# Sixty-four-row products among products of four column chunks, and GELU turned by transposes

## The chip, the cores and the metric

The kernel runs on one core of a Trainium2 chip. The metric is the device time of one execution in microseconds (us); lower is better. The engines of a core run side by side: TensorE (PE in the profile, its weight loads are PEld), VectorE (DVE), ScalarE (ACT), GpSimd (POOL) and SyncE (SP), which here issues all transfers.

## The reference, cut to what matters

One decode step for four tokens of width 448: an attention block over a cached window, then an MLP. All numbers are float32.

```python
x = A_x                                              # (4, 1, 448)
h = x + attention(layernorm(x), k_cache, v_cache, wq, wo)   # last 1024 of 4096 keys, 16 heads, 8 kv heads
y = layernorm(layernorm(h))
u = gelu(y @ w1 + b1)                                # (4, 1792), tanh form
out = h + u @ w2 + b2                                # (4, 448)
```

## The kernel before, in words

The host packs all weights and caches so that SP can fetch them in the order of their use as a few large transfers (`LOADS`, then `v7`, `wo67`, `w1`, `w2`, `w2_low`), into a ring of three buffers. The order of TensorE's instructions is that of the program text; the other engines' queues follow the program's order too, with semaphores between engines set by the tile framework.

For each of the eight key-value heads the kernel projects the queries (`project_q`), forms scores (`scores`), turns the exponentials (`transpose_p`), multiplies with the values (`values`) and adds the head's output to the output projection (`project_o`). After the last head only four rows of 448 numbers are left, and the MLP works on them in a layout of its own: a matrix with four rows is cut into four chunks of columns, chunk j stands on partitions 32 j to 32 j + 31, and of each such 32 partitions every eighth (GAP) carries a token. A product for chunk j thus writes 32 partitions of PSUM only and uses 32 columns of TensorE's array; products for four chunks can be under way at one time. Each float32 product appears in the trace as two passes (a transpose as one), so counts of matmuls there are twice those in the program.

The MLP's steps, with their lines:

- L452 to L457: `pu`, the product of the normalized tokens with w1, four row blocks (a = 0 to 3) times four chunks (j). The block a = 3 has only 64 rows.
- L468, L469: scale and bias on DVE and GELU on ACT, in two parts of the columns (256 and 192), result in `u` (128 x 448).
- L471: five matmuls on zeros (`keep_warm`), which only keep TensorE busy.
- L472 to L476: `put`, five products of column blocks of `u` with `rows_of`, which picks from the identity the 16 partitions that carry tokens. This turns GELU's result from rows into columns. The last 64 columns go to both halves of the partitions.
- L477 to L480: four DVE copies bring `put` into `gT`, where every eighth column of a block of 32 carries a token and the rest stay zero. `gT[:, c]` is the stationary operand for chunk c of w2's rows.
- L481 to L496: `py`, the product with w2. Chunks c = 0 to 10 with four column chunks j each (L486); then four products of 64 rows (L489), whose weights came by `w2_low` and all of which write column chunk j = 3 (`py[3 * Q :, 0, :]`); then chunks c = 11 to 13 (L493), of which c = 12 and 13 have three column chunks only.
- L498, L499: `res`, the sum with the residual on DVE, and the transfer of the result.

w2 comes in five pieces (L374 to L380): chunks 0 to 7 (1792 KB), chunks 8 to 10 (672 KB), the two `w2_low` halves, chunks 11 and 12 (416 KB), chunk 13 (192 KB).

Of the kernel before, what the change touches and what calls it, by code (L numbers as in the profile page):

```python
# [8 lines left out]
F32 = mybir.dt.float32  # L9
# [6 lines left out]
B, D = 4, 448  # L16
# [4 lines left out]
P = 128  # L21
H = P // 2
ND = 4
NKC = W // P
NFC = F // P
FQ = F // 4
Q = 32
# [37 lines left out]
W2L = NFC * D - 2 * (D - DW)  # L65
# [4 lines left out]
def block_kernel(ctx: ExitStack, tc, first, streams, v7, wo67, w1, w2, w2_low, out):  # L70
    nc = tc.nc
# [3 lines left out]
    once = ctx.enter_context(tc.tile_pool(name="once", bufs=1))  # L75
# [3 lines left out]
    ps_m = ctx.enter_context(tc.tile_pool(name="ps_m", bufs=2, space=PSUM))  # L79
# [51 lines left out]
    ident = const.tile([P, P], F32, name="ident")  # L131
# [27 lines left out]
    rows_of = ident.rearrange("p (j b e) -> p j b e", j=4, b=B)[:, :, :, 0]  # L159
# [3 lines left out]
    gT = const.tile([P, NFC + 2, Q], F32, name="gT")  # L163
# [7 lines left out]
    def spread(t):  # L171
        return t[..., ::GAP]
# [43 lines left out]
    def scores(g):  # L216
        s = [ps_s.tile([P, 512], F32, tag="s", name=f"s{g}_{h}") for h in range(2)]
        mx = work.tile([P, 2], F32, tag="mx", name=f"mx{g}")
        for h in range(2):
            for c in range(2):  # L220
                for b in range(B):
                    nc.tensor.matmul(  # L222
                        s[h][b * Q : (b + 1) * Q, :], qT[g % 2][:, c, b, :], load_k(g, h, c)[:, b, :],
                        start=(c == 0), stop=(c == 1),
                    )
            nc.vector.reduce_max(mx[:, h : h + 1], s[h], axis=AX.X)  # L226
        nm = work.tile([P, 1], F32, tag="nm", name=f"nm{g}")
        nc.vector.tensor_max(nm, mx[:, 0:1], mx[:, 1:2])
        nc.vector.tensor_scalar_mul(nm, nm, -SCALE)  # L229
        p = work.tile([P, 2 * 512], F32, tag="p", name=f"p{g}")  # L230
        sums = work.tile([P, 2], F32, tag="sums", name=f"sums{g}")
        for h in range(2):
            nc.scalar.activation(  # L233
                p[:, h * 512 : (h + 1) * 512], s[h], AF.Exp, bias=nm, scale=SCALE,
                accum_out=sums[:, h : h + 1],
            )
        rec = work.tile([P, 1], F32, tag="rec", name=f"rec{g}")
        nc.vector.tensor_add(rec, sums[:, 0:1], sums[:, 1:2])
        nc.vector.reciprocal(rec, rec)
        return p, rec  # L240
# [30 lines left out]
    def columns(t, j):  # L271
        if j < 3:
            return t[:, j * P : (j + 1) * P].rearrange("p (i c) -> p i c", i=2)
        return t[:, None, 3 * P :].to_broadcast([t.shape[0], 2, H])

    def heads(g, po, rec):
        o = work.tile([P, 2, DH], F32, tag="o", name=f"o{g}")
        nc.vector.tensor_scalar_mul(o[:, :, :P], po[:, :, :P], rec)  # L278
        nc.scalar.mul(o[:, :, P:], po[:, :, P:], rec)  # L279
        pt = ps_m.tile([P, 512], F32, tag="m", name=f"pot{g}")  # L280
        if g in (HKV - 3, HKV - 1):
            keep_warm(3 if g == HKV - 1 else 5, pt)
        for c in range(2):
            for i in range(2):
                at = (2 * i + c) * P - i * REP
                nc.tensor.transpose(pt[:, at : at + P], o[:, i, c * P : (c + 1) * P], ident)  # L286
        if g >= HKV - 2:
            keep_warm(1)
        dst = oT[g % 2].rearrange("p (r c) (b e) -> p r (c b) e", r=REP, b=B)[..., 0]
        src = pt.rearrange("p (i k q) -> p q k i", i=2, q=Q)[:, :REP]  # L290
        nc.vector.tensor_reduce(dst, src, axis=AX.X, op=ALU.add)
# [57 lines left out]
    p, rec = scores(0)  # L349
    project_q(1, wq_parts(part("q", 1)))  # L350
    transpose_p(0, p)
    for g in range(HKV):
        if g + 1 < HKV:
            p, rec_next = scores(g + 1)
            if g == HKV - 2:
                heads(g - 1, *late)
            if g + 2 < HKV:
                project_q(g + 2, wq_parts(part("q", g + 2)))
            transpose_p(g + 1, p)
            if g + 1 == HKV - 1:  # L360
                keep_warm(2, ps_m.tile([P, 512], F32, tag="m", name="wait"))
                tail.append(ps_t.tile([P, 2, 512], F32, tag="t", name="tail"))
                keep_warm(5)
        else:
            v7t = load_v7()
            tw = slot("w1")
            wo_last = [wo_rows(tw[:, i * WC : (i + 1) * WC]) for i in range(2)]
            nc.sync.dma_start(tw[:, : 2 * WC], wo67)
            tw1 = tw[:, 2 * WC : 2 * WC + W1C]
            for a, n in ((0, 2 * F), (2 * F, W1C - 2 * F)):  # L370
                nc.sync.dma_start(tw1[:, a : a + n], w1[:, a : a + n])
            tw2 = slot("w2")
            at = 0
            for n in (8 * D, 3 * D, 0, D + DW, DW):  # L374
                if n:
                    nc.sync.dma_start(tw2[:, at : at + n], w2[:, at : at + n])
                else:
                    for h in range(2):
                        nc.sync.dma_start(tw2[h * Q : (h + 1) * Q, W2L : W2L + 4 * H], w2_low[h, :, : Q // 8, :])
                at += n  # L380
        if g == HKV - 1:
            keep_warm(5)
        po = values(g, v7t if g == HKV - 1 else None)
        if g == HKV - 2:
            project_o(g - 1, wo_rows(part("o", g - 1)))
        if g == HKV - 3:
            late = po, rec
        else:
            heads(g, po, rec)
        if g < HKV - 3:  # L390
            project_o(g, wo_rows(part("o", g)))
        if g == HKV - 2:
            accs = once.tile([P, D], F32, tag="u", name="accs")
            nc.scalar.copy(accs, acc)
            hsum = ps_s.tile([P, 512], F32, tag="s", name="hsum")[:, :P]
            ph = hsum.rearrange("p (i c) -> p i c", i=2)
            pu = ps_s.tile([P, 512], F32, tag="s", name="pu")[:, :FQ]
            for j in range(4):
                nc.tensor.matmul(ph[j * Q : (j + 1) * Q], sel, columns(accs, j), start=True, stop=False)
        if g == HKV - 1:  # L400
            keep_warm(5)
            for i in range(2):
                project_o(HKV - 2 + i, wo_last[i])
        if g + 1 < HKV:
            rec = rec_next

    w1t = [tw1[:, a * F : (a + 1) * F] for a in range(3)] + [tw1[:, 3 * F :]]
    w2t = [tw2[:, c * D - max(c - 12, 0) * (D - DW) :][:, : D if c < 12 else DW] for c in range(NFC)]
# [21 lines left out]
    m = row_mean(hs, pm[:, 0:1], "m")  # L430
# [8 lines left out]
    m = row_mean(ds, pm2[:, 0:1], "m2")  # L439
# [8 lines left out]

    r1 = stat("r1")
    s = stat("r2")  # L450
    u = once.tile([P, FQ], F32, tag="u", name="u")
    for a in range(ND):  # L452
        for j in range(4):
            rows, w = w1_part(a, j)
# [14 lines left out]
        nc.scalar.activation(u[:, cols], u[:, cols], AF.Gelu_apprx_tanh)  # L469

    keep_warm(5)  # L471
    put = ps_m.tile([P, 4, 4, B], F32, tag="m", name="put")  # L472
    for c in range(3):
        nc.tensor.matmul(put[:, c], u[:, c * P : (c + 1) * P], rows_of, start=True, stop=True)
    for rows in (slice(0, H), slice(H, P)):
        nc.tensor.matmul(put[rows, 3], u[:, 3 * P :], rows_of, start=True, stop=True)  # L476
    dst = gT[:, :12, :].rearrange("p (c j) q -> p c j q", c=3)  # L477
    nc.vector.tensor_copy(spread(dst), put[:, :3])
    for i, rows, at in ((0, slice(0, H), 12), (1, slice(H, P), 12), (1, slice(0, H), NFC)):
        nc.vector.tensor_copy(spread(gT[rows, at : at + 2, :]), put[rows, 3].rearrange("p (j i) q -> p j i q", i=2)[:, :, i, :])  # L480
    py = ps_o.tile([P, 2, H], F32, tag="o", name="py")  # L481
    for c in range(11):
        for j in range(4):
            n = 2 if c == 0 or j < 3 else 1
            w = columns(w2t[c], j) if n == 2 else w2t[c][:, None, 3 * P :]
            nc.tensor.matmul(py[j * Q : (j + 1) * Q, :n, :], gT[:, c, :], w, start=(c == 0), stop=False)  # L486
    for i, c in enumerate((12, NFC, 13, NFC + 1)):
        w = tw2[:H, W2L + i * H : W2L + (i + 1) * H]
        nc.tensor.matmul(py[3 * Q :, 0, :], gT[:H, c, :], w, start=False, stop=False)  # L489
    for c in range(11, NFC):  # L490
        for j in range(4 if c == 11 else 3):
            w = columns(w2t[c], j) if j < 3 else w2t[c][:, None, 3 * P :]
            nc.tensor.matmul(  # L493
                py[j * Q : (j + 1) * Q, : 2 if j < 3 else 1, :], gT[:, c, :], w,
                start=False, stop=(c == NFC - 1 or j == 3),
            )  # L496
    res = once.tile([P, P], F32, tag="res", name="res")
    nc.vector.tensor_add(res, py.rearrange("p i c -> p (i c)"), hb)  # L498
    nc.sync.dma_start(out, res)  # L499
# [70 lines left out]
```

## Time and profile before

| | |
|---|---|
| median of 3 runs | 214.32 us (214.21 to 214.32) |
| the profiled execution | 214.25 us |
| its span in the profile | 212.5 us |
| TensorE busy (matmuls) | 143.2 us, 67% of the span |
| DVE, ACT, POOL busy | 36.8, 24.5, 5.0 us |
| share of the span on the chain that ended last | DMA 73%, PE 23%, DVE 1%, ACT 1% |
| moved from memory | 88.23 MB, 416 GB/s over the span |

The span reaches from the first to the last instruction of the profiled execution. Engines overlap, so their busy times don't add up to the span; the chain that ended last is followed back from the last instruction to what released it, step by step, and its shares do add up. The busy time of a matmul in the profile is from its start to the modelled end of its result, so matmuls in a stream overlap each other, and what one costs in a stream is the step from one start to the next.

### The profile page before, as it was taken

The page shows a single profiled execution, that of the slowest core. Times are in us where ns is not written, and L with a number is a line of the kernel's source. Part 1 is how long each engine was busy: PE and PEld are TensorE (multiplying, and loading weights), DVE is VectorE, ACT ScalarE, POOL GpSimd, SP SyncE. Part 2 cuts the span into 40 slices and gives each one's busy share as a digit, 9 for nine tenths or more (in the row PEclk, how much of TensorE's full clock was granted, in tenths as well). Part 3 has the DMA queues.
Part 4 walks back from the last instruction along what each step waited for, and adds up shares of the span by engine and source line. Part 5 has one row for each costly group of instructions (what it writes and reads, how often), then busy time and mean ns, then how long its engine had stood idle before and what let it go on. Part 6 is the DMA issues. An engine that isn't in the chain of part 4 may idle for free.

```text
span 212.5 us, 2534 instructions
## 1 busy us (share of the span) xinstructions
PE 143.2 (67%) x1095; PEld 56.4 (27%) x1095; DVE 36.8 (17%) x152; ACT 24.5 (12%) x58; POOL 5.0 (2%) x16
## 2 busy tenths in 40 slices
PE   0468805862861884870793780685599998999994
PEld 0332301220110521320122220141134433325453
DVE  1521400320130100310122011031032041101220
ACT  2011300210011100200003000030012002100310
POOL 5100000000000000000000000000000000000100
PEclk9999975896797579996589698599589999999999
DMA  7999899999989999899999989899999999999991
GB/s 297 436 406 509 361 489 435 406 445 397 489 375 474 445 395 462 375 503 410 424 456 403 467 382 478 364 479 450 421 435 421 423 414 412 410 432 424 421 383 43
DMA packets 3259, 88.44 MB, mean 416 GB/s; under 512 B 369, under 2 KB 689, under 8 KB 1073
## 3 DMA queue, kind: packets, MB, share of 16 engines
q1 hardware_dynamic: 3248, 88.30, 96.8%
q8 instruction: 8, 0.13, 0.2%
q14 instruction: 3, 0.02, 0.0%
HBM read 88.23 MB, written 0.07 MB: 416 GB/s over the span
## 4 chain that ended last, share of the span: by engine, by line
DMA 73%; PE 23%; SPq 1%; DVE 1%; issue 1%; ACT 1%; ACTq 0%
DMA stream<-stream 60%; DMA w<-w 12%; PE s L222 7%; PE po L261 4%; PE wait L346 3%; PE acc L296 2%; PE py L486 1%; PE pu L455 1%; PE pq L199 1%; PE pot L286 1%; PE ppt L247 1%; PE tail L346 1%; DVE o L278 0%; SPq L98 0%; PE py L493 0%
## 5 line engine op out<-in xcount | busy, mean ns | idle before, releaser
L222 PE MATMUL s<-stream,qT 128*32 128x512 f32 x256 | 37.5, 730 | 17.4 <-DMA stream<-stream 16.8
L261 PE MATMUL po<-stream,pT 128*32 128x512 f32 x224 | 31.7, 703 | 17.3 <-DMA stream<-stream 17.3
L222 PEld LDWEIGHTS s<-stream,qT 128*32 128x32 f32 x256 | 9.9, 132 | 42.6 <-issue 30.4
L226 DVE TENSOR_REDUCE mx<-s 128x1 f32<-128x512 f32 x16 | 11.1, 692 | 57.5 <-PE s L222 57.5
L199 PE MATMUL pq<-stream,yT 128*32 128x512 f32 (+1 forms) x80 | 10.2, 604 | 9.5 <-DMA stream<-stream 6.6
L261 PEld LDWEIGHTS po<-stream,pT 128*32 128x32 f32 x224 | 7.0, 124 | 35.1 <-DMA stream<-stream 20.2
L201 ACT COPY qs<-pq 128x512 f32<-128x512 f32 x8 | 4.7, 586 | 83.1 <-PE pq L199 83.1
L278 DVE TENSOR_SCALAR o<-po,rec 128x256 f32<-128x256 f32 x8 | 3.9, 484 | 59.9 <-PE po L261 59.9
L279 ACT ACTIVATE o<-po,rec 128x256 f32<-128x256 f32 x8 | 3.8, 474 | 74.2 <-DVE o L278 74.2
L233 ACT ACTIVATE p<-s,nm 128x512 f32<-128x512 f32 x16 | 10.9, 690 | 10.0 <-DVE nm L229 10.0
L247 PE MATMUL ppt<-ident,p 128*128 128x128 f32 x64 | 11.1, 303 | 0.4
L296 PE MATMUL acc<-stream,oT 128*32 128x448 f32 x48 | 7.3, 683 | 5.1 <-DMA stream<-stream 3.9
L207 PE MATMUL pqt<-ident,qs 128*128 128x128 f32 x32 | 6.1, 323 | 5.5 <-ACT qs L201 5.5
L286 PE MATMUL pot<-ident,o 128*128 128x128 f32 x32 | 7.2, 317 | 3.6 <-DVE o L278 3.1
L346 PEld LDWEIGHTS <-idle 128*32 128x32 bf16 x71 | 6.4, 96 | 9.4 <-issue 3.6
L199 PEld LDWEIGHTS pq<-stream,yT 128*32 128x32 f32 x80 | 4.2, 125 | 16.9 <-issue 15.7
L247 PEld LDWEIGHTS ppt<-ident,p 128*128 128x128 f32 x64 | 7.6, 152 | 3.7 <-ACT p L233 3.7
L346 PE MATMUL tail<-idle 128*32 128x512 bf16 x29 | 7.6, 381 | 0.0
L286 PEld LDWEIGHTS pot<-ident,o 128*128 128x128 f32 x32 | 3.4, 149 | 13.2 <-DVE o L278 10.5
L346 PE MATMUL wait<-idle 128*32 128x512 bf16 x30 | 6.8, 379 | 0.0
L207 PEld LDWEIGHTS pqt<-ident,qs 128*128 128x128 f32 x32 | 3.9, 160 | 10.2 <-ACT qs L201 8.5
L193 POOL TENSOR_TENSOR r<-ve_r,mhalf 128x1 f32<-128x1 f32 x2 | 1.1, 545 | 191.0 <-DVE ve_r L192 191.0
(118 smaller groups left out, 75.3 us busy)
## 6 DMA issues: line engine op xcount, KB each, us to landing
stream<-stream SPq DMA_DIRECT2D x5, 7040.0 KB, 37.2
stream<-stream SPq DMA_DIRECT2D x3, 6912.0 KB, 39.3
stream<-stream SPq DMA_DIRECT2D x2, 4992.0 KB, 16.0
stream<-stream SPq DMA_DIRECT2D x1, 7168.0 KB, 40.1
w<-w SPq DMA_DIRECT2D x2, 1792.0 KB, 22.4
v<-v SPq DMA_DIRECT2D x1, 3072.0 KB
w<-wo SPq DMA_DIRECT2D x1, 1792.0 KB, 19.5
w<-w SPq DMA_DIRECT2D x1, 1344.0 KB, 26.2
```

Source lines behind the costliest of these rows:

```text
L199: nc.tensor.matmul(pq[j * Q : (j + 1) * Q, cols], yT[:, a, :], w, start=True, stop=True)
L201: nc.scalar.copy(qs, pq)
L207: nc.tensor.transpose(pt[:, i * P : (i + 1) * P], qs[:, i * P : (i + 1) * P], ident)
L222: nc.tensor.matmul(s[h][b * Q : (b + 1) * Q, :], qT[g % 2][:, c, b, :], load_k(g, h, c)[:, b, :], start=(c == 0), stop=(c == 1),)
L226: nc.vector.reduce_max(mx[:, h : h + 1], s[h], axis=AX.X)
L233: nc.scalar.activation(p[:, h * 512 : (h + 1) * 512], s[h], AF.Exp, bias=nm, scale=SCALE, accum_out=sums[:, h : h + 1],)
L247: nc.tensor.transpose(pt[:, c, :], p[:, c * P : (c + 1) * P], ident)
L261: nc.tensor.matmul(po[b * Q : (b + 1) * Q], pT[g % 2][:, c, b, :], vt[:, :, b, :], start=(c == 0), stop=(c == NKC // 2 - 1),)
L278: nc.vector.tensor_scalar_mul(o[:, :, :P], po[:, :, :P], rec)
L286: nc.tensor.transpose(pt[:, at : at + P], o[:, i, c * P : (c + 1) * P], ident)
L296: nc.tensor.matmul(acc[i * Q : (i + 1) * Q, :], oT[g % 2][:, i, :], wt[:, i, :], start=(g == 0), stop=(g == HKV - 3),)
L346: nc.tensor.matmul(to[:Q, :512], idle[:, :Q], idle, start=True, stop=True)
```

## The change: what it does

Two edits in the MLP's second half, and a buffer made to fit.

First, `u` becomes 128 x 512, its last 64 columns set to zero by POOL (the earlier tile `accs`, which shares its buffer, grows with it). The five products with `rows_of` become five transposes against the identity: three into `put`, and two of 128 columns each into a second tile `put2`, the second of them 64 columns further left, so that the last 64 columns of `u` come out on either half of the partitions. The four copies to `gT` now pick every eighth column of the transposes, and the first of them reads `put` alone.

Second, the four 64-row products no longer stand in one block between chunks 10 and 11. One of them follows the product for j = 1 in each of the chunks c = 8, 9, 10 and 11, ahead of those for j = 2 and 3. The products for the chunks themselves are the same.

```diff
--- before.py
+++ after.py
@@ -390,7 +390,7 @@
         if g < HKV - 3:
             project_o(g, wo_rows(part("o", g)))
         if g == HKV - 2:
-            accs = once.tile([P, D], F32, tag="u", name="accs")
+            accs = once.tile([P, 4 * P], F32, tag="u", name="accs")[:, :D]
             nc.scalar.copy(accs, acc)
             hsum = ps_s.tile([P, 512], F32, tag="s", name="hsum")[:, :P]
             ph = hsum.rearrange("p (i c) -> p i c", i=2)
@@ -448,7 +448,8 @@
 
     r1 = stat("r1")
     s = stat("r2")
-    u = once.tile([P, FQ], F32, tag="u", name="u")
+    u = once.tile([P, 4 * P], F32, tag="u", name="u")
+    nc.gpsimd.memset(u[:, FQ:], 0.0)
     for a in range(ND):
         for j in range(4):
             rows, w = w1_part(a, j)
@@ -469,31 +470,31 @@
         nc.scalar.activation(u[:, cols], u[:, cols], AF.Gelu_apprx_tanh)
 
     keep_warm(5)
-    put = ps_m.tile([P, 4, 4, B], F32, tag="m", name="put")
+    put = ps_m.tile([P, 3 * P], F32, tag="m", name="put")
     for c in range(3):
-        nc.tensor.matmul(put[:, c], u[:, c * P : (c + 1) * P], rows_of, start=True, stop=True)
-    for rows in (slice(0, H), slice(H, P)):
-        nc.tensor.matmul(put[rows, 3], u[:, 3 * P :], rows_of, start=True, stop=True)
+        nc.tensor.transpose(put[:, c * P : (c + 1) * P], u[:, c * P : (c + 1) * P], ident)
+    put2 = ps_m.tile([P, 2 * P], F32, tag="m", name="put2")
+    for i in range(2):
+        nc.tensor.transpose(put2[:, i * P : (i + 1) * P], u[:, 3 * P - i * H : 4 * P - i * H], ident)
     dst = gT[:, :12, :].rearrange("p (c j) q -> p c j q", c=3)
-    nc.vector.tensor_copy(spread(dst), put[:, :3])
-    for i, rows, at in ((0, slice(0, H), 12), (1, slice(H, P), 12), (1, slice(0, H), NFC)):
-        nc.vector.tensor_copy(spread(gT[rows, at : at + 2, :]), put[rows, 3].rearrange("p (j i) q -> p j i q", i=2)[:, :, i, :])
+    nc.vector.tensor_copy(spread(dst), put.rearrange("p (c j b e) -> p c j b e", c=3, j=4, b=B)[..., 0])
+    halves = put2.rearrange("p (s j i b e) -> p s i j b e", s=2, j=2, i=2, b=B)[..., 0]
+    for side, i, rows, at in ((0, 0, slice(0, H), 12), (1, 1, slice(H, P), 12), (0, 1, slice(0, H), NFC)):
+        nc.vector.tensor_copy(spread(gT[rows, at : at + 2, :]), halves[rows, side, i])
     py = ps_o.tile([P, 2, H], F32, tag="o", name="py")
-    for c in range(11):
-        for j in range(4):
+    low = list(enumerate((12, NFC, 13, NFC + 1)))
+    for c in range(NFC):
+        for j in range(4 if c < 12 else 3):
             n = 2 if c == 0 or j < 3 else 1
             w = columns(w2t[c], j) if n == 2 else w2t[c][:, None, 3 * P :]
-            nc.tensor.matmul(py[j * Q : (j + 1) * Q, :n, :], gT[:, c, :], w, start=(c == 0), stop=False)
-    for i, c in enumerate((12, NFC, 13, NFC + 1)):
-        w = tw2[:H, W2L + i * H : W2L + (i + 1) * H]
-        nc.tensor.matmul(py[3 * Q :, 0, :], gT[:H, c, :], w, start=False, stop=False)
-    for c in range(11, NFC):
-        for j in range(4 if c == 11 else 3):
-            w = columns(w2t[c], j) if j < 3 else w2t[c][:, None, 3 * P :]
             nc.tensor.matmul(
-                py[j * Q : (j + 1) * Q, : 2 if j < 3 else 1, :], gT[:, c, :], w,
-                start=False, stop=(c == NFC - 1 or j == 3),
+                py[j * Q : (j + 1) * Q, :n, :], gT[:, c, :], w,
+                start=(c == 0), stop=(c == NFC - 1 or (c == 11 and j == 3)),
             )
+            if j == 1 and 8 <= c < 12:
+                i, at = low.pop(0)
+                w = tw2[:H, W2L + i * H : W2L + (i + 1) * H]
+                nc.tensor.matmul(py[3 * Q :, 0, :], gT[:H, at, :], w, start=False, stop=False)
     res = once.tile([P, P], F32, tag="res", name="res")
     nc.vector.tensor_add(res, py.rearrange("p i c -> p (i c)"), hb)
     nc.sync.dma_start(out, res)
```

## Rows read from the trace of the kernel before

**Rows 1.** Busy time of each engine, granted clock and DMA, by stretch of the end.
```profile
core 0: us, PE busy (x) PEld busy (x) DVE busy (x) ACT busy (x) POOL busy (x), PEclk, DMA share, GB/s
...
205.70:208.29 2.59, 2.53 (x88) 2.36 (x89) 0.34 (x2) 0.00 (x0) 0.00 (x0) 1.00 0.65 248
208.29:208.85 0.56, 0.56 (x11) 0.47 (x8) 0.00 (x0) 0.00 (x0) 0.00 (x0) 1.00 0.00 0
```
**Rows 2.** From the end of the chain that ended last: start, duration, step.
```profile
175.10 26.18 DMA w<-w
...
201.33 1.84 PE pu L455 x16
```
**Rows 3.** Timeline from GELU to the first product with w2.
```profile
203.83 0.69 ACT L469 ACTIVATE u<-u 128x256 f32<-128x256 f32 x2 [3.69 <-DVE u L468]
204.30 0.84 PE L474 MATMUL put<-ident,u 128*128 128x16 f32 x6
...
205.41 0.24 DVE L478 COPY gT<-put 128x48 f32<-128x48 f32 x1 [1.29 <-PE put L476]
205.54 0.54 DVE L480 COPY gT<-put 64x8 f32<-64x8 f32 x3
...
205.76 2.60 PE L486 MATMUL py<-w,gT 128*32 128x128 f32 x88 [0.39 <-DVE gT L480]
```
**Rows 4.** SP's issues of three pieces of w2, in narrow windows.
```profile
184.19 0.81 SPq L376 DMA_DIRECT2D w<-w  x2
...
189.50 0.33 SPq L376 DMA_DIRECT2D w<-w  x1
...
193.79 0.33 SPq L376 DMA_DIRECT2D w<-w  x1
```
**Rows 5.** The same three issues by size, with us from issue to landing.
```profile
w<-w SPq DMA_DIRECT2D x1, 1792.0 KB, 21.4
...
w<-w SPq DMA_DIRECT2D x1, 416.0 KB, 18.8
...
w<-w SPq DMA_DIRECT2D x1, 192.0 KB, 15.0
```
**Rows 6.** POOL's memset of gT, and the readers of accs: duration min/median/max ns, start.
```profile
L167 POOL MEMSET gT<- x1: 526/526/526, 2.9 to 2.9; 128x512 f32 x1
...
L399 PE MATMUL hsum<-accs,sel x8: 272/273/297, 185.0 to 185.3; 128*32 128x128 f32 x8
```
**Rows 7.** Timeline of four transposes of an earlier stage and their reader.
```profile
159.14 0.66 PE L207 MATMUL pqt<-ident,qs 128*128 128x128 f32 x4 [0.15 <-ACT qs L201]
...
159.83 0.23 DVE L210 TENSOR_REDUCE q<-pqt 128x16 f32<-128x64 f32 x1 [1.19 <-PE pqt L207]
```
**Rows 8.** Timeline around the 64-row block, in narrow windows.
```profile
208.09 0.27 PE L486 MATMUL py<-w,gT 128*32 128x128 f32 x1
...
208.29 0.30 PE L489 MATMUL py<-w,gT 64*32 64x64 f32 x2
...
208.71 0.22 PE L489 MATMUL py<-w,gT 64*32 64x64 f32 x1
208.85 0.31 PE L493 MATMUL py<-w,gT 128*32 128x128 f32 x4
...
209.76 0.29 DVE L498 TENSOR_TENSOR res<-py,hb 128x128 f32<-128x128 f32 x1 [3.69 <-PE py L493]
```
**Rows 9.** The last products by tile: duration min/median/max in ns, start.
```profile
L493 PE MATMUL py<-w,gT x20: 219/273/297, 208.9 to 209.4; 128*32 128x128 f32 x18, 128*32 128x64 f32 x2
```
**Rows 10.** Timeline of w1's last products, in narrow windows.
```profile
201.33 0.58 PE L455 MATMUL pu<-w,zT 128*32 128x448 f32 x4 [0.52 <-DMA w<-w]
...
201.73 0.56 PE L455 MATMUL pu<-w,zT 128*32 128x448 f32 x4
...
202.22 0.13 PEld L455 LDWEIGHTS pu<-w,zT 64*32 64x32 f32 x5 [0.73 <-issue]
```
**Rows 11.** The block's wait instruction in TensorE's queue: duration ns, start us.
```profile
L489 PEldq EVENT_SEMAPHORE  x1: 51/51/51, 207.5 to 207.5; - x1
```

## The prediction, on record before the result

> **What bounds the kernel now.** I read the chain that ended last first, then its end on the timeline, then the transfers that reach into that end, and at last single instructions in narrow windows. The chain's shares (DMA 73%, PE 23%) say that most of the span is transfers, but the change touches only the last 6 us. There the table by stretch [rows 1] should be read for two things: the granted clock is 1.00 (the 2.4 GHz level) throughout, and the transfers are still at 0.65 of the engines while w2's products run, and at 0.00 afterwards. So TensorE sets the end, but it starts into data that is only just arriving. On the chain [rows 2] w1's last piece lands at 175.10 + 26.18 = 201.28 and its product starts 0.05 later. Then follow GELU, the turn into columns, the copies, and the products with w2 from 205.76 [rows 3]. The profile puts that last start down to the DVE copy, done at 205.41 + 0.24 = 205.65. But w2's first piece was issued at 184.19 and took 21.4 us, so it landed at 205.59 [rows 4, 5]. Two waits end within 0.06 us of each other; removing one leaves the other.
>
> **The edit to GELU's turn.** It replaces five products (ten passes, 204.30 to the copy at 205.41) by five transposes. Four transposes of this shape took 0.66 us to the last result and their reader started 0.69 after the first [rows 7]; three can't take longer. The third needs GELU's second part, done at 203.83 + 0.69 = 204.52, hence ready for TensorE at about 204.57, when two of the transposes are through anyway. The first copy could then start by 204.30 + 0.69 = 204.99, take 0.24 (48 elements per partition, as now), and let TensorE go 0.11 after its end (205.65 to 205.76 now): 205.34, 0.42 us earlier than now. The copy now reads one element in eight; even at twice its price the start would be 205.58. Both lie ahead of w2's first piece at 205.59. So the products start 0.05 after the landing, at 205.64, at the earliest, and not later than now; I take 205.69, a little after the earliest since the queue handles several waits in turn. **Gain: 0.07 us, bounds 0 and 0.12**, of an apparent 0.4. The last three copies (0.54 together) end before 206.2 and serve products after 207.7: hidden. The memset on POOL waits for the readers of accs, which start by 185.3; 512 columns took 0.53 us there, 64 can't take more, and `u` isn't written before w1's products end, after 201.33 [rows 2, 6]. It costs nothing; if it ran late, POOL's power for the norm would queue behind it, by at most 0.53. No transfer is moved.
>
> **The edit to the 64-row products.** First the steps of a stream. From the first product at 205.76 to the start of the last 128-row pass at 208.09 lie 21 steps of a pass of four chunks (11 chunks, two passes each); the first pass after a restart takes 297 ns where the others take 273 [rows 9], so that one step is 0.024 longer: (2.33 - 0.024) / 21 = 0.11 us a step, 0.22 a chunk [rows 3, 8].
>
> Now the block [rows 8]. The last 128-row pass starts at 208.09, the first 64-row pass at 208.29: 0.20, which is 0.09 more than a step. The first two 64-row passes end at 208.29 + 0.30 = 208.59, a pass lasts 0.22, so the second starts at 208.37: 0.08. The other six steps run to 208.71: 0.057 each. Then the next 128-row pass starts at 208.85: 0.14, again 0.09 more than a step, and its own first step is 0.024 longer. Each change between 128 and 64 rows thus costs about 0.09 of standing and 0.024 of restart. No wait explains it: the wait for the two `w_low` pieces was passed at 207.5 [rows 11]. The same shows where no semaphore stands at all, in w1's product: the second 128-row pass follows the first by 0.40 (201.33 to 201.73, with a restart in it), the first 64-row pass follows after 0.49 [rows 10], 0.09 more than even a restarted step and 0.11 more than a plain one.
>
> The block as it is costs 208.85 - 208.09 = 0.76, less the 0.11 step that would stand there anyway, plus 0.024: **0.67 us** for one pair of changes and eight passes. Strewn, each of the four products brings its own pair: 0.20 + 0.08 + 0.14 + 0.024 - 0.11 = 0.334; four cost **1.34**. Net **+0.67**.
>
> Second, the order. The strewn product stands after j = 1, so the chunks' passes are cut into groups: {8: j0 j1}, then {8: j2 j3, 9: j0 j1}, {9, 10}, {10, 11}, and what is left of 11 with 12 and 13. Four products on four different column chunks start within 0.02 us of each other after a restart (four are under way in the row at 208.85), so I take it that those of two neighbouring chunks pair up likewise. Ahead of the last strewn product then stand eight full groups, one half and three mixed: twelve of 0.22 where eleven stand now, **+0.22**. Behind it the longest line is j = 2 of chunks 11, 12, 13, three products, as now (208.85 to 209.76 for DVE's sum).
>
> As a clock: first product 205.69; second pass of {8: j0 j1} at 205.69 + 0.024 + 17 x 0.11 = 207.58; each strewn product moves on by 0.20 + 0.08 + 0.14 to the next group's first pass, and that group's second pass comes 0.134 later, so the groups start at 208.00, 208.55, 209.11 and 209.66; 0.91 later DVE sums at 210.57, against 209.76. Chunk 11, needed at 209.11, has landed at 189.50 + 18.8 = 208.30, chunk 13 at 193.79 + 15.0 = 208.79 [rows 4, 5]: neither is waited for.
>
> **Sum:** -0.07 + 0.67 + 0.22 = +0.82 us. The profiled execution took 214.25 us, 1.75 of it outside its span: 215.07. Its time is 0.07 below the median shown, so I predict **215.1 us**.
>
> The Trainium skill, in TensorEngine Tiling, section Key Properties, says that changing the tiling mode, not just the tile, drains TensorE; the trace agrees, with 0.09 at each change [rows 8, 10]. TensorE: Matmul & The Clock Gate, section Single matmul latency, has a drain at about 175 ns; as an estimate from that page, six more changes at 0.175 would make 1.05, and the sum +1.20, 215.45 us. I keep the price of the rows.
>
> **The rivals.**
> *The strewn products run beside the others* (the other side). The column chunk j = 3 has half as many columns as the others, so it has about 0.11 us to spare in each chunk's 0.22, and a 64-row product needs 0.11. If a change of rows let the other column chunks run on and cost nothing itself, the products would vanish into that gap. Chunk 11 would be reached at 205.69 + 0.024 + 22 x 0.11 = 208.13, before its landing at 208.30; from 208.35 two chunks lead to 208.79, where chunk 13 has just landed; its first pass at 208.84 leaves 0.45 to DVE's sum, as now (0.91 less two chunks): 209.29, 0.47 earlier, **213.8 us**. w2's arrival, not TensorE, then sets the gain. For it: four chunks do run side by side. Against: both places where the row count changes stand still for 0.09, and it decides at that price being zero; at about 0.13 us in all per strewn product it breaks even. Chance 0.10. TensorE: Matmul & The Clock Gate, Part 3: Packing small matmuls, has tiles of the array run at the same time and weight loads pulled ahead where row groups don't conflict, which would favour this rival; at 208.29 the trace shows the contrary [rows 8].
>
> *Only column chunk 3 stands.* The strewn products cost 0.334 each there, the other chunks run on: chunk 3 ends its stream at 205.69 + 0.024 + 8 x 0.22 + 4 x (0.11 + 0.334) = 209.25, its last pass starts 0.06 before. Now the last pass starts at 208.85 + 0.024 + 5 x 0.11 = 209.42, 0.34 ahead of DVE's sum; so the sum comes at 209.53, 0.23 earlier, **214.0 us**. Against it speaks that the block's exit stops the passes of all four. Chance 0.06.
>
> *The halves don't pair up.* If j2 j3 of one chunk and j0 j1 of the next run one after the other, each of four groups takes one to two more steps: 0.44 to 0.88 more, 215.5 to 216.0, **215.7 us**. For it: the four now starting together belong to one chunk; against: the streams of the column chunks drift apart freely. Chance 0.14.
>
> **How the numbers follow.** The forecast has 0.70; its own range is 214.8 to 215.4 (start bounds, roundings of 0.01 in some twenty steps, 0.1 between executions). A measurement of this kernel can tell about 0.2%, 0.43 us, from no change: 213.89 to 214.75. Slower: 0.70 + 0.14 = 0.84. Rival one lies at the edge, half of it counts as faster (0.05), half as same; rival two is same with a little faster: same 0.10, faster 0.06. Range 214.5 to 215.8: it holds the forecast and most of the 0.14, and leaves out both rivals below and the end of the third.
>
> **What would show it.** Right: the first product with w2 at about 205.7, put down to w2's transfer or close behind its landing, with TensorE idle for 0.3 us or more before it; four 64-row products each with 0.20 before and 0.14 behind; DVE's sum near 210.6. Wrong: 64-row passes that overlap those of other chunks in time with no gap before them; a first start well before 205.6, which would mean that w2 landed earlier than its row says; or a granted clock below 1.00 in the last 5 us, where it has been 1.00 so far.

## The result, and the profile after

The changed kernel takes 215.18 us (median of 6, 215.14 to 215.33) against 214.32 us (median of 6, 214.21 to 214.5): 1.0039 times as long, 95% interval 1.0029 to 1.005. That is slower by 0.86 us, where 0.8 was forecast. Its profiled execution took 215.22 us with a span of 213.4.

The end of its timeline (start, duration, engine, line, operation, count, idle time before and what ended it) answers to [rows 3, 8]; lines from L452 on have moved by one or more.

```profile
204.37 0.60 PE L475 MATMUL put<-ident,u 128*128 128x128 f32 x3
...
205.00 0.24 DVE L480 COPY gT<-put 128x48 f32<-128x48 f32 x1 [0.81 <-PE put L475]
205.22 0.55 DVE L483 COPY gT<-put 64x8 f32<-64x8 f32 x3
...
205.80 2.16 PE L490 MATMUL py<-w,gT 128*32 128x128 f32 x68 [0.62 <-DVE gT L483]
207.89 0.13 PEld L497 LDWEIGHTS py<-w,gT 64*32 64x32 f32 x2 [0.20 <-issue]
207.89 0.30 PE L497 MATMUL py<-w,gT 64*32 64x64 f32 x2
208.12 0.16 PEld L490 LDWEIGHTS py<-w,gT 128*32 128x32 f32 x8
208.12 0.43 PE L490 MATMUL py<-w,gT 128*32 128x128 f32 x8
208.47 0.14 PEld L497 LDWEIGHTS py<-w,gT 64*32 64x32 f32 x2 [0.20 <-issue]
...
209.06 0.14 PEld L497 LDWEIGHTS py<-w,gT 64*32 64x32 f32 x2 [0.20 <-issue]
...
209.64 0.13 PEld L497 LDWEIGHTS py<-w,gT 64*32 64x32 f32 x2 [0.20 <-issue]
...
209.86 0.84 PE L490 MATMUL py<-w,gT 128*32 128x128 f32 x16
210.74 0.29 DVE L499 TENSOR_TENSOR res<-py,hb 128x128 f32<-128x128 f32 x1 [4.97 <-PE py L490]
```

Two things are to be seen. The transposes are through early: the first copy starts 0.63 after the first transpose (205.00 - 204.37), where the products took 1.11 [rows 3], but the first product with w2 comes at 205.80, no earlier than before. And the weight loads of the four 64-row products each stand 0.20 us with no wait behind it ("issue"), where one load did before, that of the block:

```profile
208.29 0.19 PEld L489 LDWEIGHTS py<-w,gT 64*32 64x32 f32 x3 [0.20 <-issue]
```

The period from one strewn product to the next is 0.58. From the first product to DVE's sum it is now 210.74 - 205.80 = 4.94 us, where it was 209.76 - 205.76 = 4.00.

By stretch, granted clock and transfers (columns as in [rows 1]):

```profile
205.80:207.89 2.09, 2.09 (x68) 1.89 (x68) 0.00 (x0) 0.00 (x0) 0.00 (x0) 1.00 0.73 277
207.89:209.86 1.97, 1.97 (x34) 1.01 (x32) 0.00 (x0) 0.00 (x0) 0.00 (x0) 1.00 0.07 26
```

The clock stays at 1.00. In the stretch of the strewn products TensorE's matmuls look fully busy (1.97 of 1.97), although seven of the eight changes between 128 and 64 rows, each with its gap, lie in it: their modelled ends overlap the gaps. The weight loads show it: 1.01 of 1.97, where they were 1.89 of 2.09.

### The profile page after: what moved, and what is told of

Its sections match the earlier page's. It is cut to its first block, busy times and chain, and to the rows that moved or that the text cites. A ratio compares the mean times of both kernels' runs of the same rounds, so it can differ in the third digit from the quotient of the medians.

```text
span 213.4 us, 2526 instructions
## 1 busy us (share of the span) xinstructions
PE 143.6 (67%) x1090; PEld 55.7 (26%) x1090; DVE 36.9 (17%) x152; ACT 24.5 (11%) x58; POOL 5.2 (2%) x17
## 4 chain that ended last, share of the span: by engine, by line
DMA 72%; PE 22%; DVE 3%; ACT 1%; issue 1%; SPq 0%; ACTq 0%
DMA stream<-stream 57%; DMA w<-w 12%; PE s L222 5%; PE po L261 5%; PE pq L199 2%; DMA stream<-first 2%; PE py L490 2%; PE pqt L207 1%; PE acc L296 1%; PE pu L456 1%; PE ppt L247 1%; ACT qs L201 1%; PE tail L346 1%; DVE o L278 0%; ACT o L279 0%
## 5 line engine op out<-in xcount | busy, mean ns | idle before, releaser
L222 PE MATMUL s<-stream,qT 128*32 128x512 f32 x256 | 38.1, 741 | 20.4 <-DMA stream<-stream 19.8
L261 PE MATMUL po<-stream,pT 128*32 128x512 f32 x224 | 29.5, 663 | 15.4 <-DMA stream<-stream 15.4
L199 PE MATMUL pq<-stream,yT 128*32 128x512 f32 (+1 forms) x80 | 11.2, 657 | 9.6 <-DMA stream<-stream 6.7
L210 DVE TENSOR_REDUCE q<-pqt 128x16 f32<-128x64 f32 x8 | 1.8, 225 | 19.2 <-PE pqt L207 19.2
```

Source lines behind the costliest of these rows:

```text
L199: nc.tensor.matmul(pq[j * Q : (j + 1) * Q, cols], yT[:, a, :], w, start=True, stop=True)
L222: nc.tensor.matmul(s[h][b * Q : (b + 1) * Q, :], qT[g % 2][:, c, b, :], load_k(g, h, c)[:, b, :], start=(c == 0), stop=(c == 1),)
L261: nc.tensor.matmul(po[b * Q : (b + 1) * Q], pT[g % 2][:, c, b, :], vt[:, :, b, :], start=(c == 0), stop=(c == NKC // 2 - 1),)
```

## The experiments

All ran beside the kernel before on the same chip; the medians given for it are of the same session. A ratio is the time over that of the kernel before, with its 95% interval. The edits are shown shortened, with "..." where code is left out.

**The strewn products alone.** The kernel before with only the second edit.

```diff
-    for c in range(11): ...; the block of four; for c in range(11, NFC): ...
+    for c in range(NFC): ...
+            if j == 1 and 8 <= c < 12:   # one 64-row product
```

> The strewn products alone, GELU turned by products with selectors as before. My theory: the whole loss is here, +0.9 us against the kernel before (0.67 for three more pairs of changes between 128 and 64 rows, 0.22 for the chunk cut in halves): 215.2 us. Rival: the transposes or their strided copies bear part of the loss: well below 215.2, towards 214.3 us if they bear all of it.

Measured: 215.32 us against 214.33, ratio 1.0046 (1.0034 to 1.0059). From the first product to DVE's sum 4.94 us, as in the changed kernel (its lines L487 and L496):

```profile
205.87 2.16 PE L487 MATMUL py<-w,gT 128*32 128x128 f32 x68 [0.39 <-DVE gT L480]
...
210.81 0.29 DVE L496 TENSOR_TENSOR res<-py,hb 128x128 f32<-128x128 f32 x1 [4.62 <-PE py L487]
```

The whole loss is in this edit.

**The transposes alone.** The changed kernel with the block of the kernel before.

```diff
-            if j == 1 and 8 <= c < 12: ...
+    for i, c in enumerate((12, NFC, 13, NFC + 1)):   # the block, between chunks 10 and 11
```

> The transposes alone, the 64-row products in one block as before. My theory: the first product with w2 waits for w2's first piece, so the earlier copies buy next to nothing: first product 0.10 to 0.15 us behind the landing, time 214.25 to 214.32 us. Rival: the turn was the bound, and the products start 0.4 us earlier: 213.9 us.

Measured: 214.36 us against 214.33, ratio 0.9999 (0.999 to 1.0008): no difference that can be told. On its timeline the first copy ends at 205.10 + 0.24 = 205.34 and the first product, which reads it, starts at 205.88, 0.54 later:

```profile
205.10 0.24 DVE L480 COPY gT<-put 128x48 f32<-128x48 f32 x1 [0.82 <-PE put L475]
205.32 0.55 DVE L483 COPY gT<-put 64x8 f32<-64x8 f32 x3
...
205.88 2.60 PE L489 MATMUL py<-w,gT 128*32 128x128 f32 x88 [0.60 <-DVE gT L483]
```

Something other than that copy holds it.

**The last three copies on ACT.** The profile names the last DVE copy (L483) as what the first product waited for, and it does end 0.01 to 0.03 us ahead of it, although chunk 0 doesn't read it.

```diff
-        nc.vector.tensor_copy(spread(gT[rows, at : at + 2, :]), halves[rows, side, i])
+        nc.scalar.copy(spread(gT[rows, at : at + 2, :]), halves[rows, side, i])
```

> The changed kernel with the last three copies to gT on ACT instead of DVE, so that DVE is done 0.5 us earlier. My theory: the first product with w2 stays 0.13 us behind the landing of w2's first piece, time 215.2 us. Rival: the profile is right to name the last DVE copy as what it waits for, and the first product comes up to 0.1 us earlier against the landing.

One execution: 215.34 us. With these three copies gone from DVE the chain of this kernel runs through w2's transfer:

```profile
184.37 21.41 DMA w<-w
205.79 0.14 issue
205.92 2.16 PE py L490 x47
```

The first product stands 0.13 us behind the landing. In the changed kernel it is the same: issued at 184.27, 21.4 under way, 205.67; first product at 205.80.

```profile
184.27 0.33 SPq L376 DMA_DIRECT2D w<-w  x1
...
w<-w SPq DMA_DIRECT2D x1, 1792.0 KB, 21.4
```

So it is w2's first piece that holds the start, and the name in the wait was a coincidence of 0.03 us.

**The strewn products at the ends of chunks.**

```diff
-            if j == 1 and 8 <= c < 12:
+            if j == 3 and 7 <= c < 11:
```

> The changed kernel with each 64-row product behind the last product of a chunk (7, 8, 9, 10) instead of in the middle of one. My theory: the four pairs of changes stay, the cut group goes, so the products from first to DVE's sum take 0.22 us less than in the changed kernel: 214.95 us. Rival: the column chunks drift across the cut at no cost, the whole loss is in the changes: as the changed kernel, 215.2 us.

Measured: 214.94 us, ratio 1.0031 (1.002 to 1.0043). Its TensorE timeline, with DVE's sum:

```profile
207.52 0.30 PE L497 MATMUL py<-w,gT 64*32 64x64 f32 x2
207.74 0.42 PE L490 MATMUL py<-w,gT 128*32 128x128 f32 x8
208.09 0.30 PE L497 MATMUL py<-w,gT 64*32 64x64 f32 x2
...
210.38 0.29 DVE L499 TENSOR_TENSOR res<-py,hb 128x128 f32<-128x128 f32 x1 [4.75 <-PE py L490]
```

The first product is at 205.64, so first product to sum is 4.74 us: 0.20 less than in the changed kernel, 0.74 more than in the kernel before. The cut chunk cost 0.20, three more pairs of changes 0.74. The medians differ by 0.24, in the same direction; the intervals of the two ratios overlap, so it is the profile, one execution of each, that tells them apart.

**The same places, without a change of rows.** The weights' other 64 rows are set to zero, so each product reads 128 rows and adds nothing more.

```diff
+            nc.gpsimd.memset(tw2[H:, W2L : W2L + 4 * H], 0.0)
...
-                w = tw2[:H, W2L + i * H : W2L + (i + 1) * H]
-                nc.tensor.matmul(py[3 * Q :, 0, :], gT[:H, at, :], w, start=False, stop=False)
+                w = tw2[:, W2L + i * H : W2L + (i + 1) * H]
+                nc.tensor.matmul(py[3 * Q :, 0, :], gT[:, at, :], w, start=False, stop=False)
```

> The changed kernel, strewn in the same places, but each of the four products reads 128 rows: the lower 64 rows of its weights are zeros, set by a memset on POOL long before. My theory: what costs is the change of the row count, so without it the four products vanish in the time that column chunk 3 has to spare, no pass waits at them, and w2's last pieces become the bound: chunk 11 about 0.1 us behind its landing, DVE's sum 0.4 us earlier than in the kernel before: 213.9 us. Rival: the cost is in the place (another product for the same 32 partitions between the others), not in the rows: 215.2 us as the changed kernel.

Measured: 213.87 us, ratio 0.9979 (0.997 to 0.9988); run once more beside the last experiment below:

> The padded kernel once more, beside the one with the columns apart on the same chip: 213.87 us as before, last piece 3.12 us behind the first.

213.82 us, ratio 0.9978 (0.9968 to 0.9987). In a narrow window of the first of these runs the strewn passes (L498) start between those of other chunks (L491), with no gap ahead of them:

```profile
207.44 0.38 PE L491 MATMUL py<-w,gT 128*32 128x128 f32 x4
207.56 0.22 PE L498 MATMUL py<-w,gT 128*32 128x64 f32 x1
207.57 0.30 PE L491 MATMUL py<-w,gT 128*32 128x128 f32 x1
207.62 0.22 PE L498 MATMUL py<-w,gT 128*32 128x64 f32 x1
...
209.28 0.29 DVE L500 TENSOR_TENSOR res<-py,hb 128x128 f32<-128x128 f32 x1 [3.54 <-PE py L491]
```

First product at 205.77, sum at 209.28: 3.51 us. Same products, same places, same order; the row count differs (and the memset, which runs long before), and 1.43 us of 4.94 are gone. The cost was the change of rows, and this version is faster than both kernels. What is left is no longer TensorE's time alone: in the second run chunk 11's weight load waits for its transfer.

```profile
208.40 0.11 PEld L491 LDWEIGHTS py<-w,gT 128*32 128x32 f32 x2 [0.17 <-DMA w<-w]
```

**No 64-row products.** The last 64 columns of chunks 12 and 13 as ordinary products of 128 rows, first within whole rows of w2, then in a transfer of their own. The last of the small copies falls away.

```diff
-            for n in (8 * D, 3 * D, 0, D + DW, DW):   # and w2_low in two halves
+            for n in (8 * D, 3 * D, 2 * D, D):
...
-        for j in range(4 if c < 12 else 3):
+        for j in range(4):
```

> The changed kernel without any 64-row product: w2's last 64 columns of chunks 12 and 13 come as part of these chunks' whole rows, and two ordinary products of 128 rows for column chunk 3 take the place of the four. The same bytes, in four pieces instead of six. My theory: with no change of rows left, w2's landings set the end, as in the padded kernel, and fewer products change nothing: 213.85 us, 0.05 either way. Rival: the four products cost column chunk 3 time in the padded kernel although they hid no change of rows, or the two w2_low transfers of 32 partitions cost the transfers more than their bytes: 213.7 us or less.

Measured: 214.05 us beside 214.35, ratio 0.9987 (0.9978 to 0.9996). Faster than before, but by less than with padding, whose ratios come from other sessions and overlap this one a little; the expected time was missed by 0.15 to 0.2 us. TensorE now waits for transfers twice:

```profile
205.70 3.63 PE L485 MATMUL py<-w,gT 128*32 128x128 f32 x112 [0.60 <-DMA w<-w]
208.35 0.37 PEld L485 LDWEIGHTS py<-w,gT 128*32 128x32 f32 x16 [0.32 <-DMA w<-w]
208.91 0.16 PEld L485 LDWEIGHTS py<-w,gT 128*32 128x32 f32 x8 [0.19 <-DMA w<-w]
```

Its first piece lands at 184.16 + 21.4 = 205.56, its last at 186.98 + 21.9 = 208.88, 3.32 us later. With padding it is 193.81 + 14.9 - (184.22 + 21.4) = 3.09, in the second run 3.20. These times to landing are rounded to 0.1; the trace's landing events give 3.31 here, and 3.12 and 3.18 with padding.

```diff
-                    for h in range(2):
-                        nc.sync.dma_start(tw2[h * Q : (h + 1) * Q, W2L : W2L + 4 * H], w2_low[h, :, : Q // 8, :])
+                    nc.sync.dma_start(tw2[:, W2L : W2L + 2 * H], w2_low)   # 128 x 128
```

> As the kernel with whole rows (two ordinary products of 128 rows for the last 64 columns), but these columns come in one transfer of their own, 128 partitions of 512 bytes, ahead of w2's last two pieces, which are as small as in the padded kernel. With whole rows the last piece landed 3.31 us behind the first, with padding 3.12, from the same bytes. My theory: the two w2_low transfers of 32 partitions cost the stream less than their bytes in whole rows do, whatever carries them, so the last piece lands 0.1 us later than in the padded kernel again: 3.2 to 3.3 us behind the first, time 213.95 to 214.05 us. Rival: what counts is how small the last two pieces are: 3.12 us, 213.85 us.

Measured: 214.14 us, ratio 0.999 (0.9981 to 0.9999), beside 213.82 with padding, all runs of the one above all of the other. The last piece lands at 189.45 + 19.5 = 208.95, 3.36 us after the first (184.19 + 21.4), by the landing events 3.35. The way is the expected one, the size somewhat more (214.05 and 3.3 at most were expected). The small last pieces alone don't bring the time back. What still differs from the padded kernel is the form of the 64 KB of low columns, there two transfers to 32 partitions each, and with it when the last piece is issued (193.81 there, 189.45 here). In the trace each of those two transfers also reports its landing in 8 events, where every other piece has 16. Which of these lets the stream end earlier there, and how, stays open.

**One wait less at the start.** The kernel with whole rows, and a small product ahead of w2's, which takes over the wait for the copies.

```diff
+    nc.tensor.matmul(tail[0][:Q, 0, :H], gT[:, 12, :], ident[:, :H], start=True, stop=True)
     for c in range(NFC):
```

> The kernel with whole rows, and one small product of a copied column of gT with the identity ahead of w2's products, into PSUM that nobody reads, so that TensorE has seen the copies before w2's first piece lands. My theory: 0.13 us lie between the landing and the first product because TensorE works off several waits in turn; with one left it falls to about 0.05 (as after w1's last piece), and the products start 0.08 us earlier; the time moves by less than 0.1 us, since w2's last pieces set the end. Rival: 0.13 us is the last copy's doing, or the price of a landing itself, and nothing moves.

Measured: 214.11 us, ratio 0.9987 (0.9978 to 0.9995), the same as without it. The trace's landing events for w2's first piece are at 205.567 without and 205.631 with the extra product; the first products start at 205.70 and 205.68. The lag falls from 0.13 to 0.05, as expected, and chunk 11 then waits the longer (0.38 in place of 0.32). Without the extra product a wait instruction of its own (51 ns) stands in TensorE's queue ahead of the first weight load; with it there is none. The line of the run without it:

```profile
L485 PEldq EVENT_SEMAPHORE  x1: 51/51/51, 205.6 to 205.6; - x1
```

Nor is 0.13 the last copy's doing: in the kernel with whole rows the copies are done by 205.49, 0.2 ahead of the first product.

## Why the prediction was right, point by point

**The start.** Forecast: held by w2's first piece, gain 0.07 with bounds 0 and 0.12. The mechanism held. The size was near the lower bound: in the profiled executions the start came 0.04 later (205.76 to 205.80), with the transfers themselves about 0.07 later (w1's product at 201.33 and 201.40), so the gain is 0.02 to 0.03. Against the run with the strewn products alone, which keeps the old turn and starts 0.19 after the landing (205.682 by its event, 205.87), it is 0.05. The step that was mis-sized is "0.05 after the landing at the earliest", taken from w1's piece; here it is 0.13, with a wait instruction and a second wait ahead of the product, and 0.05 in the run with one wait less. The guess that several waits in turn cost a little was right, and too small.

**The changes of rows.** Forecast: 0.20, 0.08, 0.14 around each strewn product, +0.67 for all. Measured: the same gaps (0.20 before each, 208.12 - 207.89 = 0.23 for the two passes and the way back), +0.74 in the run at the chunks' ends. The padded run shows that the rows are the cause and not the place.

**The cut group.** Forecast +0.22, measured +0.20. The four products after a strewn one, two of one chunk and two of the next, do pair up as assumed: a narrow window of the changed kernel shows four passes under way at once.

```profile
207.97 0.22 PE L497 MATMUL py<-w,gT 64*32 64x64 f32 x1
208.12 0.32 PE L490 MATMUL py<-w,gT 128*32 128x128 f32 x4
```

The four take 0.32 where one takes 0.30, so their starts lie within 0.02 us. Together 4.94 - 4.00 = 0.94 from first product to sum, forecast 0.67 + 0.22 = 0.89. Each period was 0.58 instead of 0.55; the run without cut groups has 0.57. Most of that is the 0.02 over which a group's four starts are spread: the way back ends at the first of them and the next step counts from the last, which the forecast's sum leaves out.

**The number.** The start gained 0.02 instead of 0.07, and the products took 0.94 more instead of 0.89: two misses of 0.05 the same way, so +0.92 in place of +0.82. The two profiled executions differ by 215.22 - 214.25 = 0.97, with the transfers 0.07 later in the changed kernel's. That the medians differ by 0.86, so close to the forecast, is in part luck of a few hundredths.

**The rivals.** Strewn products running beside the others, stopped by w2's landings, were put at 213.8 us; without a change of rows that is what happens (213.87 and 213.82). Its condition failed in the changed kernel, its arithmetic was right. That only column chunk 3 stands is ruled out by the timeline: no pass of any chunk starts between 207.69, the last before the first strewn product, and 208.12, but the strewn ones. That the halves don't pair up is ruled out by the four passes at 208.12, and by the period: one or two steps of 0.11 more would make the forecast's 0.55 into 0.66 to 0.77.

The last two 128-row starts ahead of the first strewn product, in a narrow window of the changed kernel:

```profile
207.69 0.27 PE L490 MATMUL py<-w,gT 128*32 128x128 f32 x1
207.89 0.24 PE L497 MATMUL py<-w,gT 64*32 64x64 f32 x1
```

The Trainium skill's rule in TensorEngine Tiling, section Key Properties, that a change of tiling mode drains TensorE, is borne out by the pair of runs with and without the change of rows: 0.35 us for each strewn product ((0.74 + 0.67) / 4, the 0.67 being the prediction's price of the block) against no gap with padding. The estimate from the Trainium skill's TensorE: Matmul & The Clock Gate, section Single matmul latency, 215.45 us, was further off than that from the rows; the section speaks of one matmul's latency, not of a change of mode.

## What to carry to other kernels

Before small products are strewn into gaps of a stream, look whether they have the row count of the stream: here a change of rows stopped all four column chunks, and padding with zero rows cost nothing that shows where the change cost 0.35 us a product. (It had room: column chunk 3 has half the columns of the others.) Where two waits end within a few hundredths of a microsecond of each other, an edit that removes one is worth what the other leaves; read the landing from issue and time to landing, since the profile names only one of the two. And put expensive changes of shape together, in one block, when they can't be avoided.

## What the runs showed of the hardware that I had not expected

The price of a landing at TensorE depends on what else is waited for: 0.13 us from landing to first product with several waits at the same instruction, 0.05 with one. And with the same bytes, w2's last piece landed 0.1 to 0.2 us later when the low columns came spread over 128 partitions (3.28, 3.31 and 3.35 us from the first landing to the last in the three traces, by the landing events) than with two transfers to 32 partitions (3.12 and 3.18 with padding, 3.15 to 3.18 in the other kernels that have them); the cause is open.
